# Pass order and piece widths by token group on TensorE, and a last output projection taken chunk by chunk

## The chip, the cores and the metric

One core of one Trainium2 chip. The metric is device time in microseconds; what is told of the kernel before is the median of its runs, and one profiled execution.

## The reference, cut to what matters

```python
def _B_ref(x, w1, w2):
    h = jnp.einsum("bsd,df->bsf", x, w1)
    h = _silu(h)
    return jnp.einsum("bsf,fd->bsd", h, w2)

x = A_x                                   # (1, 2048, 640)
xn = _layernorm(x, axis=-1)
s = _A_ref(xn, A_wqkv, A_wo)              # 32 heads of 20; each token attends to 8 tokens, 2 apart; then @ wo
g = _silu(_B_ref(xn, B_w1, B_w2))         # 640 -> 1536 -> 640
return x + s * g
```

The attention multiplies the normalised tokens by `wqkv` (640 x 1920), takes scores with the 8 tokens at distances 0, 2, ..., 14 back, and multiplies the result by `wo` (640 x 640).

## The kernel before, in words

The 2048 tokens are worked in four groups of 512 (two halves, and even and odd tokens in each, so that the dilated window is dense within a group). A group has four tiles of 128 tokens (`T`), the 640 features are five chunks of 128 (`DC`), the 1536 hidden features twelve blocks (`FC`). Each product is made of three passes: an operand is split into a rounded high part and the low part that is left (`TH`/`TL` for activations, `SH`/`SL` for hidden activations, `wh`/`wl` for weights), and high x high, low x high and high x low are summed in one PSUM bank. All of these operands have the type fp32r. The order of the three passes is a choice.

Per group, TensorE works in this order:

- **qkv_phase**: four quarters of eight heads; a quarter's weights are 480 columns wide (q, k and v of 160 each). Each quarter takes four PSUM banks, one for each token tile, over five chunks; lines 586 to 588 are the three passes. ScalarE then copies each bank out (`evac_qkv`, lines 419 and 422: k and v, then q), and VectorE makes the scores, the softmax and the weighted values. From group 1 on, transposes of the attention output of the group ahead (`o_chunk`, line 408) lie between chunks.
- **wo_phase**: the output projection of the group ahead. 640 output columns don't fit in a bank of 512, so `tm_banks` takes four banks for columns 0 to 383 (`CA`), one a tile, and two banks for columns 384 to 639 (`CB`), each shared by two tiles; `tm_mm` issues the two pieces (lines 620 and 622), and each piece is a matmul with a weight load of its own. `tm_views` gives the banks to whoever reads them.
- **ffn_phase**: for each of the twelve blocks the first product (lines 737 to 739, 512 tokens wide, 15 matmuls), ScalarE's two SiLU activations (lines 743 and 744), VectorE's low part, and one step later the second product, in pieces of 384 and 256 as above. At the end ScalarE applies SiLU to the six banks into the gate `G` (line 776).

After group 3, `wo_last` does the last output projection tile by tile: all three passes over five chunks for one tile, pass outside and chunk inside, so that tiles can be finished and stored one after another; the last 256 columns of the last tile go to another bank (line 709).

The accumulation banks (`acc`, six) are handed out in rotation by `bank()`; the transposes and the first product use two others (`rot`). Weights come through a ring of seven buffers.

A planner (`Weave`) is told each piece of work with its engine, a modelled duration, what it reads and writes, and a priority or due time. TensorE's work keeps the order in which it is added; the other engines' work and the DMA issues are put in an order by a simulation with these durations. `mm(n)` is the modelled duration of a matmul of n columns, and `TM` that of a 384 + 256 pair. The keys `("g", t, 0)` and `("g", t, CA)` stand for the two column ranges of a tile's gate.

Of the kernel before, what the change touches and what calls it, by code (L numbers as in the profile page):

```python
# [22 lines left out]
T = 4  # L23
# [141 lines left out]
def local_attention_silu_ffn(ctx: ExitStack, tc: tile.TileContext, x, wqkv, wo, w1, w2, out):  # L165
# [57 lines left out]
    def bank():  # L223
        i = take("acc", 6)
        return ACC[i], ("acc", i)
# [17 lines left out]
    def pe(dur, fn, reads, writes):  # L243
        add("PE", dur, fn, reads, writes)
        clock[0] += dur
# [326 lines left out]
    def qkv_phase(g, i, io):  # L572
        for q in range(NQ):
            if g == 0 and q == 0:
                ps = first_quarter(i)
            else:
                ps = [bank() for t in range(T)]
                for c in range(DC):
                    wh, wl, kh, kl = w_next("q", q, c)
                    for t in range(T):  # L580
                        o, kp = ps[t]

                        def unit(c=c, t=t, o=o, wh=wh, wl=wl):
                            o = o[:, :3 * CQ]
                            hi, lo = TH[i][:, c, tsl(t)], TL[i][:, c, tsl(t)]
                            nc.tensor.matmul(o, hi, wh, start=c == 0, stop=False)  # L586
                            nc.tensor.matmul(o, lo, wh, start=False, stop=False)  # L587
                            nc.tensor.matmul(o, hi, wl, start=False, stop=c == DC - 1)  # L588
                        pe(3 * mm(480), unit, t_keys(i, [c], [t]) + [kh, kl], [kp])
                    w_done()  # L590
                    if g and (q, c) in O_AT:
                        o_chunk(g - 1, O_AT[q, c], io)
            if g == 0:
                add("POOL", 2.0, lambda q=q: nc.gpsimd.memset(KV[q][0:2, :, 0:HALO, :], 0.0), ["first"] if q else [],
                    [("halo", q, 1, 0), ("halo", q, 2, 0), ("halo", q, 3, 0), ("halo", q, 4, 0)], 1 + q)
            for t in range(T):
                evac_qkv(g, q, t, *ps[t])
            halo(g, q)
            scores(g, q)
            if q:  # L600
                values(g, q - 1)
        values(g, NQ - 1)
# [5 lines left out]
    OL_AT = {8: 0, 9: 1, 10: 2, 11: 3, 12: 4}  # L608
    XT_AT = 7

    def tm_banks():
        a = [bank() for t in range(T)]
        b = [bank() for t in range(T // 2)]
        return a, b

    def tm_mm(banks, t, st, w, first, last, cols=(0, 1)):
        a, b = banks
        h = t % 2
        if 0 in cols:
            nc.tensor.matmul(a[t][0][:, :CA], st, w[:, :CA], start=first, stop=last)  # L620
        if 1 in cols:
            nc.tensor.matmul(b[t // 2][0][:, h * CB:(h + 1) * CB], st, w[:, CA:], start=first and h == 0,  # L622
                             stop=last, skip_group_check=True)

    def tm_views(banks):

        a, b = banks
        for k in range(T // 2):
            for t in (2 * k, 2 * k + 1):
                yield a[t][0][:, :CA].rearrange("p (t m) -> p t m", t=1), a[t][1], slice(t, t + 1), slice(0, CA)  # L630
            yield b[k][0].rearrange("p (t m) -> p t m", t=2), b[k][1], slice(2 * k, 2 * k + 2), slice(CA, D)

    def gkeys(ts, cs):
        return [("g", t, cs.start) for t in range(ts.start, ts.stop)]

    TM = mm(CA) + mm(CB)

# [25 lines left out]
    def wo_last(g, i):  # L663

        banks = tm_banks()
        a, b = banks
        lastb, klast = rot()
        ws = [w_next("wo", c) for c in range(DC)]
        kw = [k for w in ws for k in w[2:]]
        tk = t_keys(i, range(DC))  # L670
        xr = [XR[t] if t < 2 else XIN[:, t, :] for t in range(T)]
        kx = [("xr", t) if t < 2 else ("xin", t) for t in range(T)]
        for t in range(T):
            dma(lambda t=t: nc.sync.dma_start(xr[t], rows(xg, g)[:, t, :]), [], [kx[t]], P * D * 4, clock[0] - 20)

        def give(p, kp, t, cs):
            n = cs.stop - cs.start
            dve(n, lambda: nc.vector.tensor_tensor(out=G[:, t, cs], in0=p, in1=G[:, t, cs], op=OP.mult),
                [kp], [("g", t, cs.start)], 0)
            dve(n, lambda: nc.vector.tensor_tensor(out=xr[t][:, cs], in0=xr[t][:, cs], in1=G[:, t, cs], op=OP.add),  # L680
                [("g", t, cs.start)], [kx[t]], 0, lock=True)

        def leave(t, cs):
            dma(lambda: nc.sync.dma_start(rows(og, g)[:, t, cs], xr[t][:, cs]), [kx[t]], [], P * 4 * (cs.stop - cs.start), 0)

        def whole(t, cols):
            for k in range(3):
                for c in range(DC):
                    st = (TH, TH, TL)[k][i][:, c, tsl(t)]
                    tm_mm(banks, t, st, ws[c][k == 1], k + c == 0, k == 2 and c == DC - 1, cols)  # L690

        A, B = slice(0, CA), slice(CA, D)
        for t in range(T - 1):
            pe(15 * TM, lambda t=t: whole(t, (0, 1)), tk + kw, [a[t][1], b[t // 2][1]])
            give(a[t][0][:, :CA], a[t][1], t, A)
            if t:
                for u in range(t // 2 * 2, t + 1):
                    give(b[t // 2][0][:, u % 2 * CB:(u % 2 + 1) * CB], b[t // 2][1], u, B)
                    leave(u, slice(0, D))
        t = T - 1  # L700
        pe(15 * mm(CA), lambda: whole(t, (0,)), tk + kw, [a[t][1]])
        give(a[t][0][:, :CA], a[t][1], t, A)
        leave(t, A)

        def rest():
            for k in range(3):
                for c in range(DC):
                    st = (TH, TH, TL)[k][i][:, c, tsl(t)]
                    nc.tensor.matmul(lastb[:, :CB], st, ws[c][k == 1][:, CA:], start=k + c == 0, stop=k == 2 and c == DC - 1)  # L709
        pe(15 * mm(CB), rest, tk + kw, [klast])  # L710
        give(lastb[:, :CB], klast, t, B)
        leave(t, B)

    def ffn_phase(g, i, ix, io):
        nxt = g + 1 if g + 1 < NG else None
        ps = prev = None
        for f in range(FC + 1):
# [11 lines left out]
            if f < FC:  # L729
                wh, wl, kh, kl = w_next("w1", f)  # L730
                h, kp = rot()
                s = f % 2

                def first(wh=wh, wl=wl, h=h):
                    for c in range(DC):
                        cs = tsl(c)
                        nc.tensor.matmul(h, wh[:, cs], TH[i][:, c, :], start=c == 0, stop=False)  # L737
                        nc.tensor.matmul(h, wh[:, cs], TL[i][:, c, :], start=False, stop=False)  # L738
                        nc.tensor.matmul(h, wl[:, cs], TH[i][:, c, :], start=False, stop=c == DC - 1)  # L739
                pe(15 * mm(TOK), first, t_keys(i, range(DC)) + [kh, kl], [kp])  # L740
                w_done()
                sf, sh, sl = SF[s], SH[s], SL[s]
                act(TOK, lambda sh=sh, h=h: nc.scalar.activation(sh, h, AF.Silu), [kp], [("sh", s)], 0, "silu")  # L743
                act(TOK, lambda sf=sf, h=h: nc.scalar.activation(sf, h, AF.Silu), [kp], [("sf", s)], 0, "silu")
                dve(TOK, lambda sf=sf, sh=sh, sl=sl: nc.vector.tensor_tensor(
                    out=sl, in0=sf, in1=sh.bitcast(F32), op=OP.subtract), [("sf", s), ("sh", s)], [("sl", s)], 0, lock=True)
                cur = sh, sl, ("sh", s), ("sl", s)
            if nxt is None and f in OL_AT:
                o_chunk(g, OL_AT[f], io)
            if f:  # L750
                sh, sl, ksh, ksl = prev
                if ps is None:
                    ps = tm_banks()
                a, b = ps
                wh, wl, kh, kl = w_next("w2", f - 1)
                for t in range(T):
                    def big(t=t, f=f, wh=wh, wl=wl, sh=sh):
                        tm_mm(ps, t, sh[:, tsl(t)], wh, f == 1, False)
                        tm_mm(ps, t, sh[:, tsl(t)], wl, False, False)

                    def small(t=t, f=f, wh=wh, sl=sl):
                        tm_mm(ps, t, sl[:, tsl(t)], wh, False, f == FC)
                    ko = [a[t][1], b[t // 2][1]]
                    pe(2 * TM, big, [ksh, kh, kl], ko)
                    if f == FC:
                        pe(TM, small, [ksl, kh], ko)
                    else:
                        late.append((TM, small, [ksl, kh], ko))
                for args in late:
                    pe(*args)  # L770
                late.clear()
                w_done()
# [47 lines left out]
```

## Time and profile before

| | |
|---|---|
| median of 3 runs | 645.65 us (645.18 to 646.17) |
| profiled execution | 645.26 us |
| its span, first to last instruction | 643.5 us |
| granted TensorE clock, mean | 1.000 |
| TensorE busy | 636.0 us (99%), 3502 matmuls |
| weight loads | 576.1 us (90%), 3502 |
| VectorE busy | 539.0 us (84%) |
| ScalarE, GpSimd busy | 206.7 us (32%), 115.2 us (18%) |
| DMA | 162.44 MB, mean 252 GB/s |

The span lies inside the time of the execution; the rest is launch and end. Matmuls overlap their neighbours, so the busy time of TensorE says that it is occupied, and its pace is read from one start to the next. In rows by line, "out<-in" names the tile written and those read, then partitions x elements.

### The profile page before, as it was taken

What the parts mean: (1) busy time and instruction counts of PE and PEld (TensorE: products, weight loads), DVE (VectorE), ACT (ScalarE), POOL (GpSimd) and SP (SyncE); (2) the same over time, 40 slices, a digit from 0 to 9 for tenths busy, and PEclk for the clock granted to TensorE, in tenths of its full rate; (3) what the DMA queues carried; (4) which work ended last, traced back from release to release, by engine and by line L of the source; (5) the groups of instructions that cost most, each with busy time, mean ns of one, the idle gap of its engine ahead of it and who ended that gap; (6) DMA issues with size and microseconds to landing.
All of it is one profiled execution on the core that took longest, in us unless ns stands there. A gap on an engine that the chain in (4) does not pass through costs nothing.

```text
span 643.5 us, 9030 instructions
## 1 busy us (share of the span) xinstructions
PE 636.0 (99%) x3502; PEld 576.1 (90%) x3502; DVE 539.0 (84%) x532; ACT 206.7 (32%) x401; POOL 115.2 (18%) x171
## 2 busy tenths in 40 slices
PE   7999999999999999999999999999999999999997
PEld 6888899999888989999888999999988899899997
DVE  5699999999899989998949999999106999999714
ACT  5436453443534023324332112223313222233130
POOL 7410000001100341111211124111111113311100
PEclk9999999999999999999999999999999999999999
DMA  9999999676999987656599978864579996876522
GB/s 275 336 303 328 325 402 394 260 233 206 301 329 323 295 288 267 185 174 212 179 266 270 297 233 252 306 189 160 170 206 263 275 301 213 300 253 203 165 83 81
DMA packets 64794, 162.44 MB, mean 252 GB/s; under 512 B 5632, under 2 KB 28384, under 8 KB 64752
## 3 DMA queue, kind: packets, MB, share of 16 engines
q0 software_dynamic: 20016, 82.58, 42.0%
q1 hardware_dynamic: 44736, 79.29, 38.9%
q8 instruction: 27, 0.44, 0.3%
q14 instruction: 15, 0.12, 0.1%
HBM read 109.55 MB, written 34.16 MB: 223 GB/s over the span
## 4 chain that ended last, share of the span: by engine, by line
PE 98%; DMA 1%; SPq 0%; DVE 0%; ACT 0%; issue 0%
PE acc L620 22%; PE acc L622 15%; PE acc L586 10%; PE acc L588 10%; PE acc L587 10%; PE rot L737 9%; PE rot L738 9%; PE rot L739 9%; PE rot L408 2%; PE acc L538 2%; DMA xin<-in_A_x_dram 1%; SPq L329 0%; PE rot L709 0%; PE rot L519 0%; DVE st L386 0%; ACT w L351 0%
## 5 line engine op out<-in xcount | busy, mean ns | idle before, releaser
L620 PE MATMUL acc<-w,sh 128*128 128x384 f32 x384 | 115.9, 339 | 0.0
L586 PE MATMUL acc<-w,th 128*128 128x480 f32 x300 | 115.2, 384 | 0.0
L588 PE MATMUL acc<-w,th 128*128 128x480 f32 x300 | 114.0, 380 | 0.0
L587 PE MATMUL acc<-w,tl 128*128 128x480 f32 x300 | 113.1, 377 | 0.0
L622 PE MATMUL acc<-w,sh 128*128 128x256 f32 x384 | 107.5, 280 | 0.0
L456 DVE TENSOR_TENSOR pr<-q,kv 128x2560 f32<-128x2560 f32 x32 | 90.3, 2821 | 10.0 <-DMA kv<-kv 9.6
L737 PE MATMUL rot<-th,w 128*128 128x512 f32 x240 | 95.5, 398 | 0.0
L738 PE MATMUL rot<-tl,w 128*128 128x512 f32 x240 | 94.1, 392 | 0.0
L739 PE MATMUL rot<-th,w 128*128 128x512 f32 x240 | 93.8, 391 | 0.0
L488 DVE TENSOR_TENSOR pr<-e,kv 128x2560 f32<-128x2560 f32 x32 | 90.3, 2821 | 0.7
L459 DVE TENSOR_REDUCE l<-pr 128x128 f32<-128x2560 f32 x32 | 90.0, 2813 | 0.2
L743 ACT ACTIVATE sh<-rot 128x512 fp32r<-128x512 f32 x48 | 28.7, 599 | 161.4 <-PE rot L739 161.3
L493 DVE TENSOR_TENSOR pr<-pr 128x1280 f32<-128x1280 f32 x64 | 76.5, 1196 | 1.1
L622 PEld LDWEIGHTS acc<-w,sh 128*128 128x128 f32 x384 | 72.2, 188 | 1.6
L620 PEld LDWEIGHTS acc<-w,sh 128*128 128x128 f32 x384 | 72.2, 188 | 1.7
L343 POOL DMA_DIRECT2D w<-half_q x52 | 28.0, 539 | 244.4 <-DVE pr L493 94.1
L343 POOL DMA_DIRECT2D w<-half_w x72 | 38.3, 533 | 183.2 <-PE acc L622 94.5
L587 PEld LDWEIGHTS acc<-w,tl 128*128 128x128 f32 x300 | 57.0, 190 | 8.2
L588 PEld LDWEIGHTS acc<-w,th 128*128 128x128 f32 x300 | 56.2, 187 | 8.6
L586 PEld LDWEIGHTS acc<-w,th 128*128 128x128 f32 x300 | 56.4, 188 | 7.6
L620 PE MATMUL acc<-w,sl 128*128 128x384 f32 x192 | 59.0, 338 | 0.0
L413 DVE TENSOR_TENSOR tl<-rot,th 128x512 fp32r<-128x512 f32 x35 | 23.9, 682 | 36.9 <-ACT th L412 36.9
(84 smaller groups left out, 1001.7 us busy)
## 6 DMA issues: line engine op xcount, KB each, us to landing
w<-half_w POOLq DMA_DIRECT2D x72, 640.0 KB, 5.5
w<-half_q POOLq DMA_DIRECT2D x52, 480.0 KB, 4.4
half_w<-w SPq DMA_DIRECT2D x24, 640.0 KB
half_q<-w SPq DMA_DIRECT2D x20, 480.0 KB
w<-half_wo POOLq DMA_DIRECT2D x15, 640.0 KB, 5.6
kv<-kv SPq DMA_DIRECT2D x16, 560.0 KB
kv<-kv SPq DMA_DIRECT2D x16, 420.0 KB
gate<-in_B_w_dram SPq DMA_DIRECT2D x16, 320.0 KB
```

Source lines behind the costliest of these rows:

```text
L456: dve(2560, lambda t=t: nc.vector.tensor_tensor(out=PR, in0=win(qq[:, t:t + 2, :], W, 0), in1=win(kv[:, 0, t:t + 2, :], W, CQ), op=OP.mult ...
L459: dve(2560, lambda t=t: nc.vector.tensor_reduce(out=l[:, t:t + 2].rearrange("p t w h -> p (t w h)"), in_=PR.rearrange("p t w (h d) -> p (t ...
L488: dve(2560, lambda t=t, v=v: nc.vector.tensor_tensor(out=PR.rearrange("p t w (h d) -> p t (w h) d", d=DH), in0=e[:, t:t + 2].rearrange("p ...
L493: dve(2 * n * CQ, lambda n=n: nc.vector.tensor_tensor(out=PR[:, :, 0:n, :], in0=PR[:, :, 0:n, :], in1=PR[:, :, n:2 * n, :], op=OP.add), [] ...
L586: nc.tensor.matmul(o, hi, wh, start=c == 0, stop=False)
L587: nc.tensor.matmul(o, lo, wh, start=False, stop=False)
L588: nc.tensor.matmul(o, hi, wl, start=False, stop=c == DC - 1)
L620: nc.tensor.matmul(a[t][0][:, :CA], st, w[:, :CA], start=first, stop=last)
L622: nc.tensor.matmul(b[t // 2][0][:, h * CB:(h + 1) * CB], st, w[:, CA:], start=first and h == 0, stop=last, skip_group_check=True)
L737: nc.tensor.matmul(h, wh[:, cs], TH[i][:, c, :], start=c == 0, stop=False)
L738: nc.tensor.matmul(h, wh[:, cs], TL[i][:, c, :], start=False, stop=False)
L739: nc.tensor.matmul(h, wl[:, cs], TH[i][:, c, :], start=False, stop=c == DC - 1)
```

## The change

The same products are computed, with the three passes in another order or in pieces of other widths, differently in each of the four groups:

| group | q/k/v product, passes | first FFN product | second FFN product, pieces |
|---|---|---|---|
| 0 | as before: hi·wh, lo·wh, hi·wl | as before | 384 + 256 as before |
| 1 | hi·wh, hi·wl, lo·wh | wh·hi, wl·hi, wh·lo for each chunk | 384 + 256; for the high half both 384 pieces first, then both 256 pieces |
| 2 | the same order, but for each chunk the pass is the outer loop and the tile the inner one | wh·hi, wh·lo, wl·hi, pass outside and chunk inside | 256 + 256 + 128 |
| 3 | the same order, reversed for odd tiles | wh·hi, wl·hi, wh·lo, pass outside; each matmul in two halves of 256 tokens | 512 + 128 |

In groups 2 and 3 the 128-column pieces of all four tiles share one bank, so that the second FFN product takes five banks, not six (`tm_banks(1)`), and `tm_views` and `gkeys` follow. The output projections keep 384 + 256 and six banks. In `wo_last` the loops of pass and chunk are exchanged in `whole`. The durations told to the planner are unchanged.

```diff
-                    for t in range(T):
+                    for t, part in [(t, (k,)) for k in range(3) for t in range(T)] if g == 2 else [(t, range(3)) for t in range(T)]:
...
-                            nc.tensor.matmul(o, hi, wh, start=c == 0, stop=False)
-                            nc.tensor.matmul(o, lo, wh, start=False, stop=False)
-                            nc.tensor.matmul(o, hi, wl, start=False, stop=c == DC - 1)
-                        pe(3 * mm(480), unit, t_keys(i, [c], [t]) + [kh, kl], [kp])
+                            p = [(hi, wh), (hi, wl), (lo, wh)] if g else [(hi, wh), (lo, wh), (hi, wl)]
+                            if g == 3 and t % 2:
+                                p = p[::-1]
+                            for k in part:
+                                nc.tensor.matmul(o, *p[k], start=c + k == 0, stop=c == DC - 1 and k == 2)
+                        pe(len(part) * mm(480), unit, t_keys(i, [c], [t]) + [kh, kl], [kp])
...
-    def tm_banks():
+    def tm_banks(lay=0):
         a = [bank() for t in range(T)]
-        b = [bank() for t in range(T // 2)]
+        b = [bank() for t in range(T // 2 if lay == 0 else 1)]
         return a, b
...
+    PIECES = [[(0, 384), (384, 640)], [(0, 384), (384, 640)], [(0, 256), (256, 512), (512, 640)], [(0, 512), (512, 640)]]
+
+    def tm_b(banks, t):
+
+        a, b = banks
+        n = T // len(b)
+        return b[t // n], t % n
+
+    def tm_mm(banks, t, st, w, first, last, cols=(0, 1), pieces=PIECES[0]):
+        a, b = banks
+        edge = pieces[-1][0]
+        (pb, _), h = tm_b(banks, t)
+        for k, (c0, c1) in enumerate(pieces):
+            if c0 < edge:
+                if 0 in cols:
+                    nc.tensor.matmul(a[t][0][:, c0:c1], st, w[:, c0:c1], start=first and c0 == 0, stop=last,
+                                     skip_group_check=True)
+            elif 1 in cols:
+                n = c1 - c0
+                nc.tensor.matmul(pb[:, h * n:(h + 1) * n], st, w[:, c0:c1], start=first and h == 0,
+                                 stop=last, skip_group_check=True)
...
         def whole(t, cols):
-            for k in range(3):
-                for c in range(DC):
+            for c in range(DC):
+                for k in range(3):
                     st = (TH, TH, TL)[k][i][:, c, tsl(t)]
                     tm_mm(banks, t, st, ws[c][k == 1], k + c == 0, k == 2 and c == DC - 1, cols)
...
                 def first(wh=wh, wl=wl, h=h):
-                    for c in range(DC):
-                        cs = tsl(c)
-                        nc.tensor.matmul(h, wh[:, cs], TH[i][:, c, :], start=c == 0, stop=False)
-                        nc.tensor.matmul(h, wh[:, cs], TL[i][:, c, :], start=False, stop=False)
-                        nc.tensor.matmul(h, wl[:, cs], TH[i][:, c, :], start=False, stop=c == DC - 1)
+                    steps = [(c, k) for c in range(DC) for k in range(3)] if g < 2 else [(c, k) for k in range(3) for c in range(DC)]
+                    for n, (c, k) in enumerate(steps):
+                        w = (wh, wh, wl)[k] if g % 2 == 0 else (wh, wl, wh)[k]
+                        x = (TH, TL, TH)[k] if g % 2 == 0 else (TH, TH, TL)[k]
+                        for a in range(0, TOK, 256 if g == 3 else TOK):
+                            b = a + (256 if g == 3 else TOK)
+                            nc.tensor.matmul(h[:, a:b], w[:, tsl(c)], x[i][:, c, a:b], start=n + a == 0,
+                                             stop=n == 14, skip_group_check=True)
                 pe(15 * mm(TOK), first, t_keys(i, range(DC)) + [kh, kl], [kp])
...
                 if ps is None:
-                    ps = tm_banks()
+                    ps = tm_banks(int(g > 1))
...
                     def big(t=t, f=f, wh=wh, wl=wl, sh=sh):
-                        tm_mm(ps, t, sh[:, tsl(t)], wh, f == 1, False)
-                        tm_mm(ps, t, sh[:, tsl(t)], wl, False, False)
+                        if g == 1:
+                            for k in range(2):
+                                tm_mm(ps, t, sh[:, tsl(t)], wh, f == 1, False, (k,))
+                                tm_mm(ps, t, sh[:, tsl(t)], wl, False, False, (k,))
+                            return
+                        tm_mm(ps, t, sh[:, tsl(t)], wh, f == 1, False, pieces=PIECES[g])
+                        tm_mm(ps, t, sh[:, tsl(t)], wl, False, False, pieces=PIECES[g])
 
                     def small(t=t, f=f, wh=wh, sl=sl):
-                        tm_mm(ps, t, sl[:, tsl(t)], wh, False, f == FC)
+                        tm_mm(ps, t, sl[:, tsl(t)], wh, False, f == FC, pieces=PIECES[g])
```

More of the change, by code (lines that the diff above doesn't have):

```diff
@@ L579, in qkv_phase, with unit @@
                     wh, wl, kh, kl = w_next("q", q, c)
-                    for t in range(T):
+                    for t, part in [(t, (k,)) for k in range(3) for t in range(T)] if g == 2 else [(t, range(3)) for t in range(T)]:
                         o, kp = ps[t]
-                        def unit(c=c, t=t, o=o, wh=wh, wl=wl):
+                        def unit(c=c, t=t, o=o, wh=wh, wl=wl, part=part):
                             o = o[:, :3 * CQ]
                             hi, lo = TH[i][:, c, tsl(t)], TL[i][:, c, tsl(t)]
-                            nc.tensor.matmul(o, hi, wh, start=c == 0, stop=False)
-                            nc.tensor.matmul(o, lo, wh, start=False, stop=False)
-                            nc.tensor.matmul(o, hi, wl, start=False, stop=c == DC - 1)
-                        pe(3 * mm(480), unit, t_keys(i, [c], [t]) + [kh, kl], [kp])
+                            p = [(hi, wh), (hi, wl), (lo, wh)] if g else [(hi, wh), (lo, wh), (hi, wl)]
[4 more added lines that the diff above has]
+                        pe(len(part) * mm(480), unit, t_keys(i, [c], [t]) + [kh, kl], [kp])
                     w_done()
@@ L609, in local_attention_silu_ffn @@
     XT_AT = 7
-    def tm_banks():
+    def tm_banks(lay=0):
         a = [bank() for t in range(T)]
-        b = [bank() for t in range(T // 2)]
+        b = [bank() for t in range(T // 2 if lay == 0 else 1)]
         return a, b
-    def tm_mm(banks, t, st, w, first, last, cols=(0, 1)):
+    PIECES = [[(0, 384), (384, 640)], [(0, 384), (384, 640)], [(0, 256), (256, 512), (512, 640)], [(0, 512), (512, 640)]]
+    def tm_b(banks, t):
         a, b = banks
[L618 to L623, printed above, removed]
+        n = T // len(b)
+        return b[t // n], t % n
@@ L625, in tm_views @@
     def tm_views(banks):
         a, b = banks
[L628 to L631, printed above, removed]
+        n = T // len(b)
+        e = D - TOK // n
+        for k in range(len(b)):
+            for t in range(n * k, n * (k + 1)):
+                yield a[t][0][:, :e].rearrange("p (t m) -> p t m", t=1), a[t][1], slice(t, t + 1), slice(0, e)
+            yield b[k][0].rearrange("p (t m) -> p t m", t=n), b[k][1], slice(n * k, n * (k + 1)), slice(e, D)
@@ L633, in gkeys @@
     def gkeys(ts, cs):
-        return [("g", t, cs.start) for t in range(ts.start, ts.stop)]
+        return [("g", t, a) for t in range(ts.start, ts.stop) for a, b in ((0, CA), (CA, D)) if cs.start < b and a < cs.stop]
     TM = mm(CA) + mm(CB)
@@ L757, in big @@
                     def big(t=t, f=f, wh=wh, wl=wl, sh=sh):
-                        tm_mm(ps, t, sh[:, tsl(t)], wh, f == 1, False)
-                        tm_mm(ps, t, sh[:, tsl(t)], wl, False, False)
+                        if g == 1:
[5 more added lines that the diff above has]
+                        tm_mm(ps, t, sh[:, tsl(t)], wl, False, False, pieces=PIECES[g])
                     def small(t=t, f=f, wh=wh, sl=sl):
-                        tm_mm(ps, t, sl[:, tsl(t)], wh, False, f == FC)
-                    ko = [a[t][1], b[t // 2][1]]
+                        tm_mm(ps, t, sl[:, tsl(t)], wh, False, f == FC, pieces=PIECES[g])
+                    ko = [a[t][1], tm_b(ps, t)[0][1]]
                     pe(2 * TM, big, [ksh, kh, kl], ko)
```

## The prediction, made before the result

> **What bounds the kernel now.** I read the page first, then what each engine waited for, then the chain that ended last, then the order of TensorE's instructions in single stages.
>
> ```profile
> span 643.5 us, 9030 instructions
> PE 636.0 (99%) x3502; PEld 576.1 (90%) x3502; DVE 539.0 (84%) x532; ACT 206.7 (32%) x401; POOL 115.2 (18%) x171
> ...
> PE 98%; DMA 1%; SPq 0%; DVE 0%; ACT 0%; issue 0%
> ```
>
> The first two lines are the span and the busy times, the third the shares of the chain. TensorE carries 98% of the path that sets the end, and each of its 3502 matmuls has a weight load of its own. What did it wait for? These are all the rows for it, and one for its weight loads:
>
> ```profile
> PE rot L519 <- DVE xin L398: 1.5, 1, 1.5
> PE rot L511 <- POOL ident masks.py:199: 1.4, 1, 1.4
> ...
> PE acc L538 <- ACT w L351: 0.9, 1, 0.9
> ...
> PEld acc L622 <- ACT q L422: 0.8, 3, 0.3
> ```
>
> The three TensorE waits sum to 3.8 us, all in the first quarter's lines (511, 519, 538), which the diff leaves alone. The last row matters below: three times a weight load of line 622 waited for ScalarE's copies out of a bank. So the time is what TensorE's list of matmuls takes, start to start; busy times can't give that, since neighbours overlap. I take it from the order of starts in one step of the feed-forward (start, duration, both in us):
>
> ```profile
> 88.34 0.39 PE L737 MATMUL rot<-th,w 128*128 128x512 f32 x1
> ...
> 91.55 0.39 PE L739 MATMUL rot<-th,w 128*128 128x512 f32 x1
> 91.78 0.34 PE L620 MATMUL acc<-w,sh 128*128 128x384 f32 x1
> 91.95 0.28 PE L622 MATMUL acc<-w,sh 128*128 128x256 f32 x1
> 92.06 0.34 PE L620 MATMUL acc<-w,sh 128*128 128x384 f32 x1
> ...
> 95.17 0.28 PE L622 MATMUL acc<-w,sl 128*128 128x256 f32 x1
> 95.29 0.39 PE L737 MATMUL rot<-th,w 128*128 128x512 f32 x1
> ```
>
> Fifteen 512-wide matmuls lie between 88.34 and 91.78: 3.44 / 15 = 229 ns each. Twelve pairs of 384 + 256 lie between 91.78 and 95.29: 3.51 / 12 = 293 ns a pair, of which a 256 piece is some 0.117 (91.95 to 92.06; the finer starts scatter by 2 ns) and a 384 piece 0.176. A run of 256-wide pieces alone stands at the end of the chain:
>
> ```profile
> 638.06 1.74 PE rot L709 x15
> ```
>
> 1.74 / 15 = 116 ns. Since TensorE never waits, each nanosecond that the change adds to its list is paid in full, and other engines gain slack.
>
> **The change part by part.** The planner is told the old prices (TM, and 15 matmuls of 512), so it puts other engines' work in nearly the same order; what moves is TensorE's own list and which banks are used.
>
> *Second FFN product, group 2* (256 + 256 + 128 in place of 384 + 256). Pairs affected: 12 blocks of hidden features x 4 tiles x 3 passes = 144. The price of a 128-wide piece, p, is what the trace lacks: no product in it is narrower than 256. From below: 512 columns take 229 ns and 384 take 176, so 128 columns more cost 53; a piece that pays only for its columns costs that. From above: 128-wide transposes (from the chain, and from TensorE's order of starts) and the weight loads behind them (from its order of loads).
>
> ```profile
> 591.77 0.44 PE rot L408 x4
> ```
>
> ```profile
> 599.01 0.60 PE L408 MATMUL rot<-ident,o 128*128 128x128 f32 x4
> ```
>
> ```profile
> 599.34 0.19 PEld L620 LDWEIGHTS acc<-w,sh 128*128 128x128 f32 x1
> 599.45 0.19 PEld L622 LDWEIGHTS acc<-w,sh 128*128 128x128 f32 x1
> ```
>
> Four transposes of 128 columns take 0.44, 110 ns each: as long as a 256-wide product nearly, though they stream half as many columns. And after them two product weight loads start 0.11 apart. That is what a weight load would give that can't be finished sooner and that only one matmul can hide. The 116 ns row bounds it: there one load per 116 ns goes through. I take p = 110, the row nearest in width; up to 116 adds 288 x 6 ns = 1.7 us for both groups. Then a triple is 117 + 117 + 110 = 344, less 293: +51 ns x 144 = **+7.3 us**.
>
> *Second FFN product, group 3* (512 + 128): 229 + 110 - 293 = +46 ns x 144 = **+6.6 us**. A 512 piece gains nothing by the narrow neighbour: the load that follows the narrow one is what the neighbour can't hide.
>
> *First FFN product, group 3*: each 512-wide matmul becomes two of 256, 12 x 15 = 180 times: 2 x 116 - 229 = +3 ns, **+0.5 us**. Bounds: 114 to 118 a piece, -0.2 to +1.3.
>
> *Order of the passes* (query/key/value product in groups 1 to 3, first product in 1 to 3, group 1's pieces). Same matmuls in another order. Does a start cost more when the next matmul goes to another bank, or meets another operand?
>
> ```profile
> 319.93 0.38 PE L588 MATMUL acc<-w,th 128*128 128x480 f32 x1
> 320.15 0.38 PE L586 MATMUL acc<-w,th 128*128 128x480 f32 x1
> 320.37 0.38 PE L587 MATMUL acc<-w,tl 128*128 128x480 f32 x1
> ```
>
> 588 to 586 crosses to the next tile's bank, 586 to 587 stays: 0.22 both. I take zero, within 2 ns x 500 matmuls = 1 us either way.
>
> *Waits in group 2.* There the pass is the outer loop, the tile the inner one, so all four tiles end within the last four matmuls of a quarter, not one every three. Six banks rotate, four a quarter: the next quarter's tiles 2 and 3 take the banks of tiles 0 and 1. This is the same end of a quarter as it is now, before the output projection of the group ahead, on TensorE and on ScalarE:
>
> ```profile
> 359.17 0.38 PE L588 MATMUL acc<-w,th 128*128 128x480 f32 x1
> ...
> 361.12 0.38 PE L588 MATMUL acc<-w,th 128*128 128x480 f32 x1
> 361.34 0.34 PE L620 MATMUL acc<-w,th 128*128 128x384 f32 x1
> 361.57 0.39 PE L622 MATMUL acc<-w,th 128*128 128x256 f32 x1
> ```
>
> ```profile
> 359.59 0.44 ACT L419 ACTIVATE kv<-acc 128x320 f32<-128x320 f32 x1
> ...
> 360.24 0.44 ACT L419 ACTIVATE kv<-acc 128x320 f32<-128x320 f32 x1
> ...
> 361.22 0.30 ACT L422 ACTIVATE q<-acc 128x160 f32<-128x160 f32 x1
> ```
>
> Tile 0's last matmul starts at 359.17, its copy at 359.59 (0.42 later), and tiles follow every 0.65. Line 622's first piece needs tile 2's bank and starts at 361.57, right when tile 2's copy ends (361.22 + 0.30). Now call the end of the quarter T. With the new order tile 0's last matmul starts at T - 0.86, its copies run from T - 0.44 to T + 0.2, tile 1's to T + 0.85, tile 2's to T + 1.5. In the next quarter tile 2 wants tile 0's bank at T + 0.43 (free) and tile 3 tile 1's at T + 0.65: 0.2 us late, three times, **+0.7 us** (0 to 1.5, if ScalarE is in other work). Before the projection the first 256 piece waits until T + 1.5 and not T + 0.23: **+1.3 us** once. All later matmuls queue behind the waiting one, TensorE starting them in order; nobody else is harmed.
>
> *Bank count in groups 2 and 3*: the pieces of 128 share one bank, so these products take five banks. At the end of group 3 the last projection's first narrow piece then falls on tile 3's bank, whose 512-wide gate activation can't begin before that tile ends.
>
> ```profile
> L743 ACT ACTIVATE sh<-rot 128x512 fp32r<-128x512 f32 x48 | 28.7, 599 | 161.4 <-PE rot L739 161.3
> ```
>
> 599 ns for 512 columns on ScalarE: tile 3's last wide piece starts 0.34 before the end, the copy 0.42 after it, and it is done 0.7 us into the projection, which wants the bank at 0.2: **+0.5 us** (0 to 0.8).
>
> *Last projection chunk by chunk*: the same 384 + 256 pieces, chunk outside, pass inside. It needs the last chunk of the attention output later than now, and no wait of that stage is in the rows: zero, hidden by nothing that it could lose.
>
> Sum: 7.3 + 6.6 + 0.5 + 0.7 + 1.3 + 0.5 = 16.9. The profiled execution took 645.26 us (its span 643.5 and 1.8 around it): 662.2. The median of the runs is 645.65, 0.4 more, so I say **662.6 us**.
>
> **The rivals.**
>
> *Narrow products run at a quarter of the rate.* All product matmuls here are at least 256 wide; if under that width a column costs four times as much (the operands are 4 bytes wide), p = 4 x 53 to 4 x 56 (229 - 117 = 112 ns per 256 columns gives 56 per 128), 212 to 224 ns. Then 288 x (212 - 110) to 288 x (224 - 110) = 29 to 33 us more: 692 to 695. Against it: 128-wide fp32 transposes do not pay it. For it: no product in the trace disproves it. The Trainium skill, FP8 and Floating Point Precision, section TensorE Precision Notes, says that true FP32 makes 4 passes through the array. That the wide products here take 229 ns for 512 columns shows that they do not; the page names no width at which that would change.
>
> *A narrow piece pays for its columns alone.* If the load of the weights is taken ahead by more than one matmul, p = 53: 288 x 57 ns = 16.4 us less, 646.2, not slower as far as it can be told. The point: p under 55.6 ns puts the whole within 1.3 us of now. The place: the narrow pieces of both second products. For it: weight loads start as soon as the matmul ahead has started. Against it: the 0.44 row, and that 256 columns at 116 ns pay 10 above two times 53. The Trainium skill, TensorE: Matmul & The Clock Gate, section Back-to-back issue gap, gives N / 2.4 + 2.5 ns, 55.8 at 128 columns, for matmuls alone, and 81 for pairs with loads (131 at 512 columns). The 229 ns rows at 512 columns disagree with 131. By 81 the sum would be an estimated 654.
>
> *The order costs or saves at each matmul.* Already priced at 1 us either way; to offset 16.9 us, the 480-wide matmuls of three groups (720) would each have to save 23 ns, more than the some 21 by which a start gap of 0.22 us exceeds 480 columns at 53 ns per 128 (199). I leave it inside the forecast's range.
>
> **How the numbers follow.** A measurement of this kernel can tell 0.2% (1.3 us) from no change. Weight-load-bound p (105 to 118): 0.66. Its own range is 659 to 666: without the three waits it is 2.5 less, with p = 116 it is 1.7 more, and the order gives 1 either way. The quarter rate: 0.20. Columns alone: 0.08, of which half lies within 0.2% and a quarter below (if the waits fail to appear too). Prices in between (60 to 105): 0.06, 648 to 660. To hold 8 in 10 I take the first two, 658 to 696. Faster 0.02, same 0.04, slower 0.94.
>
> **What would show each step.** In the order of starts of group 2's second product, a narrow piece followed by the next piece 110 ns later, and 344 ns a triple; in group 3, 341 a pair and 232 for two halves of the first product. The two FFN stages, now in these windows (from, to, length, busy times),
>
> ```profile
> 378.71:464.50 85.79, 85.79 (x491) 78.32 (x490) 71.61 (x63) 25.15 (x40) 19.29 (x28) 1.00 0.66 213
> ...
> 536.05:621.75 85.70, 85.70 (x491) 78.05 (x489) 71.53 (x64) 24.71 (x40) 18.43 (x27) 1.00 0.64 212
> ```
>
> should be 7.3 us longer in group 2 and 7.1 in group 3 (DVE has 14 us to spare in each, so it sets no new bound). A wait of line 622's successor for ScalarE of about 1.3 us at the head of the projection in group 2, three of 0.2 in its quarters, one of 0.5 at the last projection. Groups 0 and 1 should keep their length within 0.5 us. Wrong it would be if a narrow piece's gap is near 55 or over 200, or if groups 0 and 1 move.

## The result and the profile after

The changed kernel takes **665.88 us** (median of 4 runs, 664.93 to 666.75) against 645.41 for the kernel before in the same comparison (645.16 to 646.17): ratio 1.0315, 95% interval 1.0296 to 1.0334. It is 20.5 us slower; the sum forecast 16.9 (662.6, range 658 to 696). The page of the profiled execution, the longest of the four (666.75):

```profile
span 665.0 us, 9671 instructions
PE 655.9 (99%) x3826; PEld 594.8 (89%) x3826; DVE 537.0 (81%) x532; ACT 204.9 (31%) x399; POOL 114.8 (17%) x171
...
PE 97%; DMA 1%; ACT 1%; SPq 0%; DVE 0%; issue 0%
```

The other engines do the same work as before, less two activations on ScalarE (two second products fill five banks, not six); TensorE has 324 matmuls more, each with a load, and is still the path. What it waited for, all rows, and the waits of its loads for the banks that matter here:

```profile
PE rot L511 <- POOL ident masks.py:199: 1.4, 1, 1.4
PE rot L519 <- DVE xin L398: 1.3, 1, 1.3
PE acc L637 <- ACT q L422: 1.0, 1, 1.0
PE acc L538 <- ACT w L351: 0.9, 1, 0.9
PE acc L637 <- ACT gate L801: 0.5, 1, 0.5
PE acc L590 <- ACT q L422: 0.2, 1, 0.2
...
PEld acc L637 <- ACT q L422: 1.8, 3, 1.3
...
PEld acc L590 <- ACT q L422: 1.3, 3, 0.6
PEld acc L637 <- ACT gate L801: 0.7, 1, 0.7
```

The three new TensorE rows are the three waits that were forecast: ahead of the projection in group 2 (1.0), at the last projection (0.5, and 0.7 for its load), in group 2's quarters (0.2 here; the loads waited there three times, 1.3 in sum, and the whole stage tells more). Lines have moved: 590 is the q/k/v product, 633 the wide pieces, 637 the narrow ones, 758 the first product, 726 the last tile's rest.

Where the time went, by stage, from the first start of one to that of the next, and for the last projection to the start of its last matmul (us):

| stage | before | after | more | forecast |
|---|---|---|---|---|
| start and group 0 | 149.81 | 150.20 | 0.4 | 0 |
| group 1: q/k/v, projection, FFN | 54.18, 17.38, 85.78 | 54.24, 18.14, 85.97 | 0.1, 0.8, 0.2 | 0 |
| group 2: q/k/v | 54.18 | 55.20 | 1.0 | 0.7 |
| group 2: projection | 17.37 | 19.18 | 1.8 | 1.3 |
| group 2: FFN | 85.78 | 93.72 | 7.9 | 7.3 |
| group 3: q/k/v, projection | 54.18, 17.37 | 54.56, 18.14 | 0.4, 0.8 | 0 |
| group 3: FFN | 85.70 | 93.74 | 8.0 | 7.1 |
| last projection | 17.76 | 17.88 | 0.1 | 0.5 |

The two FFN windows that answer to those of before:

```profile
382.93:476.65 93.72, 93.72 (x634) 86.08 (x633) 68.19 (x63) 25.08 (x39) 19.09 (x28) 1.00 0.62 195
549.34:643.09 93.75, 93.75 (x671) 87.64 (x669) 70.81 (x63) 24.66 (x39) 18.94 (x27) 1.00 0.59 192
```

**How a narrow piece reads.** The order of starts in group 2 (rows with x2 are two 256 pieces in a row), and in group 3:

```profile
431.17 0.22 PE L637 MATMUL acc<-w,sl 128*128 128x128 f32 x1
431.23 0.45 PE L633 MATMUL acc<-w,sl 128*128 128x256 f32 x2
431.51 0.22 PE L637 MATMUL acc<-w,sl 128*128 128x128 f32 x1
...
642.35 0.22 PE L637 MATMUL acc<-w,sh 128*128 128x128 f32 x1
642.41 0.44 PE L633 MATMUL acc<-w,sh 128*128 128x512 f32 x1
642.69 0.22 PE L637 MATMUL acc<-w,sh 128*128 128x128 f32 x1
```

A triple takes 431.51 - 431.17 = 0.34, a pair 642.69 - 642.35 = 0.34, as forecast (344 and 341 ns; the next two triples take 0.35). But the narrow piece seems to cost only 0.06 (642.35 to 642.41), and the wide one behind it 0.28 in place of 0.229. The weight loads of the same place say which:

```profile
642.35 0.19 PEld L633 LDWEIGHTS acc<-w,sh 128*128 128x128 f32 x1
642.46 0.19 PEld L637 LDWEIGHTS acc<-w,sh 128*128 128x128 f32 x1
642.69 0.19 PEld L633 LDWEIGHTS acc<-w,sl 128*128 128x128 f32 x1
```

The load for the wide piece starts with the narrow one (642.35), and the load after it comes 0.11 later, not 0.06: the wide piece is on record from 642.41, but the next load, which in these traces starts with the matmul ahead of it, says 642.46. So 0.11 for the narrow piece and 0.23 for the 512.

### The profile page after: what moved, and what is told of

Read it like the earlier page. It is cut to its first block, busy times and chain, and to the rows that moved or that the text cites. A ratio compares the mean times of both kernels' runs of the same rounds, so it can differ in the third digit from the quotient of the medians.

```text
span 665.0 us, 9671 instructions
## 1 busy us (share of the span) xinstructions
PE 655.9 (99%) x3826; PEld 594.8 (89%) x3826; DVE 537.0 (81%) x532; ACT 204.9 (31%) x399; POOL 114.8 (17%) x171
## 4 chain that ended last, share of the span: by engine, by line
PE 97%; DMA 1%; ACT 1%; SPq 0%; DVE 0%; issue 0%
PE acc L590 29%; PE acc L633 26%; PE rot L758 25%; PE acc L637 12%; PE rot L408 2%; PE acc L538 2%; DMA xin<-in_A_x_dram 1%; SPq L329 0%; PE rot L726 0%; PE rot L519 0%; ACT q L422 0%; DVE st L386 0%; ACT kv L419 0%; ACT gate L801 0%; ACT th L412 0%
## 5 line engine op out<-in xcount | busy, mean ns | idle before, releaser
L590 PE MATMUL acc<-w,th 128*128 128x480 f32 x600 | 165.9, 382 | 0.2 <-ACT q L422 0.2
L758 PE MATMUL rot<-th,w 128*128 128x512 f32 (+1 forms) x600 | 140.1, 351 | 0.0
L633 PE MATMUL acc<-w,sh 128*128 128x384 f32 (+2 forms) x480 | 122.2, 346 | 0.0
L758 PEld LDWEIGHTS rot<-th,w 128*128 128x128 f32 x600 | 95.1, 188 | 13.3
L590 PE MATMUL acc<-w,tl 128*128 128x480 f32 x300 | 97.6, 379 | 0.0
L637 PE MATMUL acc<-w,sh 128*128 128x256 f32 (+1 forms) x384 | 88.7, 251 | 0.0
L758 PE MATMUL rot<-tl,w 128*128 128x512 f32 (+1 forms) x300 | 78.9, 347 | 0.0
L633 PE MATMUL acc<-w,sl 128*128 128x384 f32 (+2 forms) x240 | 65.7, 347 | 0.0
L765 DVE TENSOR_TENSOR sl<-sf,sh 128x512 fp32r<-128x512 f32 x48 | 35.2, 733 | 33.5 <-ACT sf L764 33.1
L758 PEld LDWEIGHTS rot<-tl,w 128*128 128x128 f32 x300 | 48.8, 188 | 7.2
```

The lines of the kernel that those rows point to most:

```text
L590: nc.tensor.matmul(o, *p[k], start=c + k == 0, stop=c == DC - 1 and k == 2)
L633: nc.tensor.matmul(a[t][0][:, c0:c1], st, w[:, c0:c1], start=first and c0 == 0, stop=last, skip_group_check=True)
L637: nc.tensor.matmul(pb[:, h * n:(h + 1) * n], st, w[:, c0:c1], start=first and h == 0, stop=last, skip_group_check=True)
L758: nc.tensor.matmul(h[:, a:b], w[:, tsl(c)], x[i][:, c, a:b], start=n + a == 0, stop=n == 14, skip_group_check=True)
```

## The experiments

Four ask what the narrow piece pays for, three what else is in the 20.5 us, one what the last projection's new order does alone. The kernel before was measured at 645.11 beside the two halved loads, the orders alone and the last projection alone, and at 645.28 beside the other four.

**Whose load is it? First the narrow piece's own.**

```diff
+                r = 64 if n == 128 and not first else P
-                nc.tensor.matmul(pb[:, h * n:(h + 1) * n], st, w[:, c0:c1], ...
+                nc.tensor.matmul(pb[:r, h * n:(h + 1) * n], st[:, :r], w[:, c0:c1], ...
```

> The changed kernel, but each 128-wide piece (all but the first of a product) loads only 64 of its 128 stationary columns, so half of its output rows are left out. Theory A (the weight load of the NEXT matmul can't be hidden behind 128 columns): the narrow piece's own load was hidden behind the wide piece ahead, so nothing moves: 665.9 within 1. Theory B (the narrow matmul waits for its own load, or is slow by its own output size): about 50 ns x 288 = 14 us less, near 651.5. Theory C (a narrow matmul has a fixed length of some 110 ns whatever is loaded): nothing moves, 665.9.

Measured 665.69, ratio to before 1.0313 (1.0297 to 1.0328): nothing moved. Theory B falls. In group 3:

```profile
593.08 0.22 PE L638 MATMUL acc<-w,sh 128*64 128x128 f32 x1
593.14 0.45 PE L633 MATMUL acc<-w,sh 128*128 128x512 f32 x1
593.42 0.22 PE L638 MATMUL acc<-w,sh 128*64 128x128 f32 x1
```

The pair is 0.34 still, though the narrow load is half as wide (128*64).

**Or the load of the piece behind it?**

```diff
+            r = 64 if c0 == 0 and edge == 512 and not first else P
-                    nc.tensor.matmul(a[t][0][:, c0:c1], st, w[:, c0:c1], ...
+                    nc.tensor.matmul(a[t][0][:r, c0:c1], st[:, :r], w[:, c0:c1], ...
```

> The changed kernel, but the first wide piece of each tile and pass in groups 2 and 3 (the one that follows a narrow piece) loads only 64 of its 128 stationary columns, so half of its output rows are left out; the narrow pieces are whole. Theory A (the load of the next matmul sets the pace after a narrow piece): the load halves to some 55 ns and fits behind the 128 columns: about 50 ns x 288 = 14 us less, near 651.5. Theory B (own load) and theory C (fixed length of a narrow matmul): nothing moves, 665.9 within 1.

Measured 651.83, ratio 1.0101 (1.0085 to 1.0118): 13.9 us less than the experiment ahead, beside which it ran; 14 were expected. In group 3:

```profile
593.02 0.39 PE L634 MATMUL acc<-w,sh 128*64 128x512 f32 x1
593.25 0.22 PE L638 MATMUL acc<-w,sh 128*128 128x128 f32 x1
593.31 0.39 PE L634 MATMUL acc<-w,sh 128*64 128x512 f32 x1
```

A pair is 0.29: the 512 piece has its 0.23 back, and the narrow one costs 0.06, its columns. It is not slow by itself (theory C falls): it is too short to cover the next load. The piece with half a load also writes half its rows, but its 0.23 is what a 512 piece with all its rows takes in the first product (229 ns), so the time came back with the load. The Trainium skill, TensorE: Matmul & The Clock Gate, section LDWEIGHTS, says that a load takes its columns divided by 1.2 ns, which is an estimated 107 ns for 128 columns and 53 for 64. The runs agree: 0.11 between the loads above, and no stall behind 0.06 with 64.

**Does the price fall with the piece's width?** Two widths: 448 + 192 in groups 2 and 3 (with six banks), and 512 + 64 + 64 in group 3.

```diff
-[(0, 256), (256, 512), (512, 640)], [(0, 512), (512, 640)]]
+[(0, 448), (448, 640)], [(0, 448), (448, 640)]]
```

> The changed kernel with pieces of 448 + 192 columns in groups 2 and 3 and six banks. Everything but the widths of the second product gives 649.5 (orders alone) + 1.2 (halves) = 650.7. Theory A (a load of some 110 ns that can be hidden only behind the one matmul ahead of it): a pair is 448 columns at 203 ns + 110 = 313, 20 more than now, x 288 = 5.8 us: 656.5. Rival (a narrow piece has a fixed extra of 57 ns over its columns, whatever its width): 203 + 80 + 57 = 340, +13.5: 664. Rival (columns alone): 650.7.

Measured 656.66, ratio 1.0167 (1.0152 to 1.0183), 0.2 from theory A. In group 3:

```profile
573.01 0.40 PE L633 MATMUL acc<-w,sh 128*128 128x448 f32 x1
573.24 0.25 PE L637 MATMUL acc<-w,sh 128*128 128x192 f32 x1
573.33 0.39 PE L633 MATMUL acc<-w,sh 128*128 128x448 f32 x1
```

A pair is 0.32 (313 ns expected; the rivals' totals were 664 and 650.7), less than the 0.34 of 512 + 128 for the same 640 columns, since the 64 columns that left the wide piece (27 ns) now pass while the next load runs.

```diff
-[(0, 512), (512, 640)]]
+[(0, 512), (512, 576), (576, 640)]]
```

> The changed kernel with the 128-wide piece of group 3 split into two of 64 (512 + 64 + 64). Theory A: each narrow piece costs the load behind it however few columns it has, 229 + 110 + 110 = 449 in place of 340, x 144 = 15.7 us more: 681.6. Rival (cost goes with the columns): 2 x (27 + some 5) for 60 + 51, no more than 666. Rival (a fixed extra of 57 for each piece over its columns): 229 + 2 x (27 + 57) = 397, +57 x 144 = 8.2: 674.

Measured 682.87, ratio 1.0577 (1.0561 to 1.0593): 17.0 more than the changed kernel, 15.7 expected by A, 8 and 0 by the rivals. In group 3:

```profile
602.14 0.48 PE L633 MATMUL acc<-w,sh 128*128 128x512 f32 x1
602.46 0.30 PE L637 MATMUL acc<-w,sh 128*128 128x64 f32 x2
602.60 0.48 PE L633 MATMUL acc<-w,sh 128*128 128x512 f32 x1
```

0.46 for the three pieces, 0.12 more than with one narrow piece. It is again a load's time for each piece, however narrow.

**The orders alone.** All widths and bank counts as before:

```diff
-    PIECES = [[(0, 384), (384, 640)], [(0, 384), (384, 640)], [(0, 256), (256, 512), (512, 640)], [(0, 512), (512, 640)]]
+    PIECES = [[(0, 384), (384, 640)]] * 4
...
-                    ps = tm_banks(int(g > 1))
+                    ps = tm_banks()
```

(and no halves in the first product)

> The changed kernel with all widths as before (384 + 256 in every group, six banks, no halves in the first product): what is left is the pass orders, the pass-outside loops of group 2, group 1's order of pieces and the last projection chunk by chunk. My sum says only group 2's waits are left: 0.7 + 1.3 = 2.0 us over before, so 647.4. Rival (the orders themselves cost at each matmul, as the output projections' 0.8 us each in the changed kernel hint): 649 to 650.

Measured 649.55, ratio 1.0067 (1.0052 to 1.0082): 4.4 more, so the rival was nearer. In its trace the two FFN stages are back:

```profile
381.42:467.33 85.91, 85.91 (x491) 78.35 (x489) 67.90 (x63) 25.15 (x40) 19.30 (x28) 1.00 0.67 212
539.71:625.46 85.75, 85.75 (x490) 78.04 (x489) 69.24 (x63) 24.72 (x40) 19.44 (x27) 1.00 0.64 211
```

so pass order inside the products is free to within 0.13 us a stage (85.91 and 85.75 against 85.79 and 85.70). Its span is 3.7 longer than that of before: 1.0 in group 2's quarters, 1.8 in its projection, 0.8 in group 3's projection, which has no wait, and 0.4 in small shifts, less 0.2 at the start. The 0.8 is told of below. Taken from the changed kernel's FFN stages, widths cost 93.72 - 85.91 = 7.8 us in group 2, and widths and halves 93.75 - 85.75 = 8.0 in group 3.

**The waits.** The changed kernel with group 2's tile loop outside again, and the last projection's first narrow piece on the bank that is free:

```diff
-... for k in range(3) for t in range(T)] if g == 2 else [(t, range(3)) for t in range(T)]:
+... for k in range(3) for t in range(T)] if g == 9 else [(t, range(3)) for t in range(T)]:
...
-        banks = tm_banks()
+        n = [bank() for _ in range(6)]
+        banks = [n[1], n[2], n[3], n[5]], [n[0], n[4]]
```

> The changed kernel with group 2's tile loop outside again (its own passes kept) and the last projection's first narrow piece put on the bank that is free first. My reading of the two traces: 1.0 us of waits in group 2's quarters, 1.0 before the projection there and 0.6 at the last projection go: 663.3. If the waits were only cover for something else: 665.9. The pace of the projections may move it by 0.8 us either way.

Measured 663.22, ratio 1.0269 (1.0252 to 1.0286), 2.7 less than the changed kernel. By stage it is 1.0 in group 2's quarters, 1.0 in its projection, 0.7 at the end. The last two of these stages, 19.18 and 17.88 in the changed kernel, are here:

```profile
362.97:381.11 18.14, 18.14 (x121) 17.90 (x120) 17.83 (x16) 1.24 (x4) 2.65 (x5) 1.00 1.09 304
641.26:658.41 17.15, 17.15 (x122) 17.15 (x120) 6.75 (x14) 1.09 (x2) 0.00 (x0) 1.00 0.15 58
```

**The halves alone**, on the kernel before:

```diff
+                        n = 256 if g == 3 else TOK
+                        for k, (w, x) in enumerate(((wh, TH), (wh, TL), (wl, TH))):
+                            for a in range(0, TOK, n):
+                                nc.tensor.matmul(h[:, a:a + n], w[:, cs], x[i][:, c, a:a + n], ...
```

> The kernel before with only the first product of group 3 in halves of 256 tokens. The prediction had 2 x 116 - 229 = 3 ns x 180 = 0.5 us: 645.6. The changed kernel's trace has 118 a half: 6.5 ns x 180 = 1.2 us: 646.3.

Measured 646.31, ratio 1.0012 (1.0002 to 1.0021), 1.0 more. Group 3's FFN stage, 85.70 before:

```profile
536.11:622.92 86.81, 86.81 (x670) 86.81 (x669) 71.16 (x63) 24.72 (x40) 18.42 (x27) 1.00 0.65 207
```

1.1 us, 6 ns for each of 180 splits: two halves come to an estimated 118 ns each ((229 + 6) / 2), longer than the 110 of a load, so a 256 piece covers it.

**The last projection chunk by chunk alone**, on the kernel before:

```diff
-            for k in range(3):
-                for c in range(DC):
+            for c in range(DC):
+                for k in range(3):
```

> The kernel before with only the last projection taken chunk by chunk. Forecast of the prediction: no difference, 645.4 within 0.3. Rival: the pace of a 384 + 256 pair in that stage (300 ns in the kernel before, 287 in the changed one) goes with the order of its loops: 60 pairs x 13 ns = 0.8 us less, 644.6. The three other output projections are the same instructions as before: if their pair stays at 287 ns the pace follows the program; if it is 300 here, it is set by chance of the run.

Measured 645.10 against 645.11, ratio 0.9994 (0.9979 to 1.0008): no difference, as forecast. Its last projection takes 17.76 us as in the kernel before, and the pair there stays at 300 ns, so the rival falls.

None of these beats the kernel before: every part of the change that was run alone either costs or does nothing.

## Why the prediction was right, point by point

- **TensorE is the bound and pays every nanosecond.** Right: it is 97% of the chain, and the parts add up. The two profiled spans differ by 665.0 - 643.5 = 21.5 us (the medians by 20.5). Of that 15.8 are widths and halves, 2.7 the waits (as taking them out gave back), 2.3 a slower pace of three projections, less 0.6 for a quicker pace of the last one; some 1.3 are small shifts, 0.4 of it at the start.
- **The price of a narrow piece, p = 110.** Right, and the reason too: the loads are 0.11 apart, and only shortening the next load gave the time back. It came out of two weak rows (transposes at 0.44 for four, two loads 0.11 apart), which could also have told of transposes only; that they told of products too was in part luck. The kernel before shows the same pattern behind its four transposes at 599.01:

```profile
599.37 0.42 PE L620 MATMUL acc<-w,sh 128*128 128x384 f32 x1
599.63 0.28 PE L622 MATMUL acc<-w,sh 128*128 128x256 f32 x1
```

  From start to start the four take 0.36, not 0.44, and the 384 piece behind them 0.26 in place of 0.176: the missing 0.08 stands with the neighbour. So the sign of a wrong forecast that I gave, a gap near 55 behind the narrow piece, was badly put: the recorded gap is 0.06, and the missing 0.05 stands with the wide piece. The sum over a pair or triple was the right test, and it held.
- **Pieces of group 2: +7.3.** Measured 7.8: a triple averaged some 347 ns, not 344, since the loads of the 256 pieces start some 0.12 us apart there (119 to 120 ns on average), and 117 was taken. **Pieces of group 3: +6.6**: 8.0 less 1.1 for the halves is 6.9.
- **Halves: +0.5.** Measured 1.0 to 1.1; the term was mis-sized, since I took 116 ns from the last tile's row, and this stage runs at 118. It lies inside the stated bounds.
- **Waits in group 2: 0.7 + 1.3.** Measured 1.0 + 1.0. ScalarE on the changed kernel begins tile 0's copy 0.45 before the end, as worked out, and is done with tile 2 a little sooner:

```profile
363.30 0.44 ACT L419 ACTIVATE kv<-acc 128x320 f32<-128x320 f32 x1 [1.36 <-PE acc L590]
...
364.64 0.35 ACT L422 ACTIVATE q<-acc 128x160 f32<-128x160 f32 x1
```

```profile
363.75 0.33 PE L633 MATMUL acc<-w,th 128*128 128x384 f32 x1
365.04 0.39 PE L637 MATMUL acc<-w,th 128*128 128x256 f32 x1 [0.95 <-ACT q L422]
```

  The copy ends at 364.64 + 0.35 = 364.99, and the piece that needs the bank starts at 365.04, 1.29 after the stage began (T + 1.5 was forecast).
- **Last projection's bank: +0.5.** The wait is there and costs 0.7 (17.88 against 17.15 without it), as long as the load waited for the bank and more than the 0.5 of TensorE's own row. Yet the stage is only 0.1 longer, because its pairs went at 287 ns and not 300, which was not forecast; a reading of this stage's length alone would have missed the wait.
- **Order at zero, groups 1 and 0 within 0.5.** This is the step that failed, and that groups 0 and 1 move was a sign of being wrong that I gave: group 1 is 1.0 longer, 0.8 of it in a projection whose instructions the change does not touch. I had priced the order inside the products and looked for its price there; the time is in the projections behind them, 2.3 in three, less 0.6 in the last. In the orders-alone run, where group 1's projection kept its pace, it is 0.8 in each of two. In the profiled execution, 4.6 us over the sum of 16.9, the pace is 1.7; widths and halves are 1.4 more than their 14.4, small shifts 1.3, waits 0.2. Most errors went the same way, so the median, 3.3 us over the forecast, stands at the upper edge of my own range for this price (659 to 666).
- **The rivals.** The quarter rate (0.20) needed 212 ns a piece; 110 was measured, so the four passes that the Trainium skill, FP8 and Floating Point Precision, section TensorE Precision Notes, gives for true FP32 do not come in at 128 columns. Columns alone (0.08) is what the piece does when the next load is short: p = 60 in that experiment, but not in a stream with whole loads. The Trainium skill, TensorE: Matmul & The Clock Gate, section Back-to-back issue gap, gives N / 2.4 + 2.5 ns for matmuls alone, an estimated 55.8 at 128 columns, which is near the 60; its 81 for pairs with loads is not seen here, where it is 110.

## What to carry to other kernels

Where each matmul brings its own weights, a piece that is shorter than the load behind it (a load of 128 columns takes 110 ns, about as long as 256 columns of product) is paid for at the price of the load, so split 640 as 384 + 256 and not as 512 + 128. Read the price of a piece from the sum of a repeating pattern, or from the starts of the loads, not from the gap behind it: a stall stands with the neighbour. And when a loop is turned so that several accumulators end together, ask who empties their banks and which matmul wants the first and the last of them.

## What the runs showed of the hardware that I had not expected

The same 60 pairs of 384 + 256 in an output projection run at one of two steady paces. The projection in group 1, three executions: the kernel before with the last projection changed, the order-only kernel, the changed kernel (for the last two, TensorE's list up to there is the same):

```profile
203.99:221.36 17.37, 17.37 (x121) 17.14 (x120) 17.20 (x12) 3.15 (x6) 2.64 (x5) 1.00 1.10 321
```

```profile
203.82:221.19 17.37, 17.37 (x122) 17.14 (x120) 17.20 (x12) 3.03 (x6) 2.63 (x5) 1.00 1.07 337
```

```profile
204.44:222.58 18.14, 18.14 (x121) 17.90 (x120) 17.97 (x14) 3.04 (x6) 2.65 (x5) 1.00 1.13 328
```

17.37 or 18.14: within the stage the starts settle either at 171 and 116 ns (287 a pair) or at 182 and 118 (300), and then stay there. In the kernel before all three such stages go at 287 and the last projection at 300; in the changed kernel the three go at 300 and the last at 287.

Read by the starts in one trace of each kernel: in groups 2 and 3, the seven kernels with the new pass order (the changed kernel and its variants) have all fourteen such stages at 300, and the three with the old order have all six at 287. In group 1 those seven have the same list of matmuls up to the stage's end, and yet three go at 287 and four at 300, while the three with the old order go at 287. The length alone misleads here: with two pieces of 64, group 1's projection takes 18.24 us at 287 a pair, because its second piece waited for a bank:

```profile
204.27 0.34 PE L633 MATMUL acc<-w,th 128*128 128x384 f32 x1
205.37 0.39 PE L637 MATMUL acc<-w,th 128*128 128x256 f32 x1 [0.76 <-ACT q L422]
```

So the pace goes with the new pass order ahead of the stage, but in group 1 the order alone does not decide it. The 0.8 us there can't be put down to the change alone. What sets the pace stays open: no run here chose it on purpose.
